# Local attention and a three-weight maxout layer: attention products of two tiles in one insertion, four rotating banks for the unit products, respaced operand steps and a fifth output buffer

## The chip, the cores and the metric

One core of a Trainium2 chip runs the whole program. The metric is the device time of one execution in microseconds; three runs of the kernel before gave 628.42, 628.75 and 629.54 us.

## What is computed

The reference, cut to what matters (8 batches, 8 heads, 576 positions, 64 values a head; 4608 tokens of 512 values):

```python
# attention within chunks of 64 positions
scores = (q_c @ k_c.T) / sqrt(64);  attn = softmax(scores);  x = attn @ v_c
# maxout layer with a hidden width of 768, then the way out
h = max(x @ w1, x @ w2, x @ w3);    out = h @ w_out
```

Everything is float32. Large products are made of three TensorE products of rounded parts (high times low, low times high, high times high).

## The kernel before

**Tiles, groups, units.** The 4608 tokens are 36 tiles of 128. The first eight tiles form two groups of four, whose layer is computed plainly (lines 173 to 175). The other 28 tiles form four *units* of 7, 8, 7 and 6 tiles (numbers 0 to 3; `UNITS`). A unit's layer uses a seven-product scheme for 2 by 2 blocks, so half of a unit's columns (448, 512, 448, 384) is one product's width. All of a unit's products are issued at line 570.

**A unit's hidden layer** (`hidden`, nine steps: three pairs of hidden blocks times w1, w2, w3). A step has seven products of six matmuls, in the order 1, 6, 5, 2, 7, 3, 4. Four of them open a PSUM bank (1, 6, 5, 4); product 2 goes on in the bank of 1, 7 in that of 6, 3 in that of 5, once ScalarE has copied the first content out (line 584, `kept<-pm`). VectorE then reads the finished banks (lines 587 and 581), GpSimd adds copies (594, 590). After the third weight of a pair (steps 3, 6 and 9) the maxima become the operands `Y` of the way out: for each of seven combinations ScalarE writes the rounded part (line 617) and VectorE the rest (line 620).

**A unit's way out** (`project`): 14 products of nine matmuls, in the order 1, 2, 6, 7, 5, 4, 3, each twice (a and b, two halves of the output). Copies of 1 and 6 go through ScalarE (658), product 2's output too (669); the results of 7, 5, 4, 3 through VectorE (661). Outputs are staged in buffers `ao` and stored to `out_t` (653); the buffers rotate over four.

**The next unit's operands** (`operands`, `last_operands`) are made during a way out, with due times counted from 6.5 us after its start: ScalarE rounds (494), VectorE subtracts the rest (498) and makes two differences (489), GpSimd two more (489).

**Attention of a tile** (`plain_steps`): its query and key block is loaded, scores S are 16 products of 64 by 64 blocks (line 223), VectorE takes maxima and subtracts (228, 233), ScalarE the exponential (237), VectorE the sums (181 to 187), GpSimd or VectorE normalises (190), TensorE transposes T in four 128 by 128 pieces (246), ScalarE copies the result (251), and V are 16 products of 64 by 64 blocks with the values (258), which ScalarE copies into the unit's input `stage` (272). Scores and V lie in one pool `ps_s` of two banks, transposes in a bank of their own, `ps_t`.

**What sets the order.** Every step is planned at a due time on a clock `now`, which adds a constant for each three products (`STEP`, `STEP_H`) and for each insertion (`ON_PE`). What is due is issued, so each engine has one fixed order. `tiles(u, time)` inserts unit u's attention work into the products of the unit ahead: at each insertion V of tile n, S of tile n + 2 and T of tile n + 1 stand in a row. Products of the units take their banks from `places`, five in rotation (three of `ps_m`, two of `ps_u`).

Of the kernel before, what the change touches and what calls it, by code (L numbers as in the profile page):

```python
# [9 lines left out]
F32 = mybir.dt.float32  # L10
# [16 lines left out]
UNITS = [7, 8, 7, 6]  # L27
HALF = 512
# [5 lines left out]
ON_PE = {"V": 0.6, "S": 0.6, "T": 0.35}  # L34
# [29 lines left out]
def chunk_attn_maxout_kernel(  # L64
# [138 lines left out]
    def plain_steps(t, x_of, col):  # L203
# [12 lines left out]

        def scores():
            r = st["r"]
            st["s"] = s = bank_of("ps_s")[:, :, t % 2 if t < 4 else 0]
# [23 lines left out]
        def transpose():  # L243
            st["tp"] = tp = ps_t.tile([P, 4, P], F32, name="tp")
            for g in range(4):
                nc.tensor.transpose(out=tp[:, g, :], in_=st["e"][:, g].rearrange("p c k -> p (c k)"),  # L246
                                    identity=ident)

        def transposed():
            st["at"] = xs_p.tile([P, 4, P], F32, name="xs")  # L250
            nc.scalar.copy(out=st["at"], in_=st["tp"])  # L251

        def values():
            st["x"] = x = bank_of("ps_x")[:, :, t % 2] if t < 4 else bank_of("ps_s")[:, :, 1]
# [209 lines left out]
    def unit(t0, count, rooms):  # L464
# [40 lines left out]

        def last_operands():
# [66 lines left out]
        def hidden(n, loads):  # L573
# [31 lines left out]
            if w == 2:  # L605
# [33 lines left out]
        def project(loads):  # L639
# [3 lines left out]
            def store(m, name, make):  # L643
# [40 lines left out]
        return dict(operands=operands, last_operands=last_operands, load=load, load_outer=load_outer, hidden=hidden,  # L684
# [129 lines left out]
    def softmax(n, at, norm):  # L814
# [4 lines left out]
        for name, d in SOFTMAX:  # L819
            plan(at + d, 0.0, lambda name=name: steps(n)[name](*((norm,) if name == "nrm" else ())))  # L820
# [14 lines left out]

    def tiles(u, time):
# [134 lines left out]
```

## Time and profile before

| | |
|---|---|
| median of three runs | 628.75 us |
| the profiled execution | 628.41 us, its span 626.6 us |
| TensorE busy | 613.3 us (98%), weight loads 532.9 us (85%) |
| VectorE, GpSimd, ScalarE busy | 71%, 45%, 44% |
| DMA | 161.26 MB, 73% of the 16 engines' span |
| the chain that ended last | TensorE 82%, VectorE 10%, ScalarE 3% |

The share of TensorE says that it has nearly always a product under way; how long it waited shows only where a product starts later than its spacing to the one ahead. The chain of work gives the places: where it leaves TensorE, another engine held it up.

### The profile page before, as it was taken

Reading aid. Unit: us, or ns where it says so; the run is one execution under the profiler, and the core shown is the slowest. Engines: PE = TensorE matmul, PEld = TensorE weight load, DVE = VectorE, ACT = ScalarE, POOL = GpSimd, SP = SyncE. Lnnn points to the kernel's source line nnn. Section 1 sums busy time; section 2 is a strip of 40 time slices with the busy share of each in tenths; the row PEclk is TensorE's granted clock in tenths of the full one; section 3 lists DMA queues with packets and bytes.
Section 4 is the critical chain, followed back from the end, with each engine's and each line's share of the span. In section 5 each row is a group of like instructions: output and inputs, shape, how many; then the busy total and the mean of one; then the engine's idle time right before and its main releaser. Section 6 shows DMA issues by size and latency. Waiting matters only on the chain.

```text
span 626.6 us, 12688 instructions
## 1 busy us (share of the span) xinstructions
PE 613.3 (98%) x5101; PEld 532.9 (85%) x5102; DVE 446.7 (71%) x684; ACT 272.7 (44%) x483; POOL 281.4 (45%) x235
## 2 busy tenths in 40 slices
PE   7899999999999899999999999999999999999997
PEld 3888888887888789998888888788989999999997
DVE  5898964788756878688659596885488668375752
ACT  4888634345444535353425252533243354232340
POOL 2423577765355765444334443452354334243430
PEclk9999999999999999999999999999999999999999
DMA  8978558685979988575966665759765566977774
GB/s 334 371 291 295 206 186 337 205 282 186 339 230 310 360 308 337 168 259 177 413 244 225 230 203 172 241 190 388 252 223 199 200 200 209 374 263 247 236 233 170
DMA packets 54219, 161.26 MB, mean 257 GB/s; under 512 B 4880, under 2 KB 17168, under 8 KB 49168
## 3 DMA queue, kind: packets, MB, share of 16 engines
q1 hardware_dynamic: 54160, 160.45, 73.0%
q8 instruction: 40, 0.66, 0.4%
q14 instruction: 19, 0.16, 0.1%
HBM read 128.97 MB, written 31.46 MB: 256 GB/s over the span
## 4 chain that ended last, share of the span: by engine, by line
PE 82%; DVE 10%; ACT 3%; issue 3%; DMA 1%; POOL 1%; DVEq 0%; ACTq 0%; POOLq 0%
PE pm L570 57%; PE pm L173 6%; PE pm L174 6%; PE pm L175 6%; PE s L258 3%; PE tp L246 2%; PE s L223 2%; DVE e L233 1%; DVE X L498 1%; DMA out_t<-ao 1%; DVE mx L228 1%; PE pm L736 1%; DVE s L384 1%; DVE sm L181 1%; DVE most L581 1%
## 5 line engine op out<-in xcount | busy, mean ns | idle before, releaser
L570 PE MATMUL pm<-X,ring 128*128 128x448 f32 (+2 forms) x1512 | 311.2, 365 | 2.9 <-ACT kept L584 2.3
L570 PEld LDWEIGHTS pm<-X,ring 128*128 128x128 f32 x1512 | 276.8, 188 | 30.2 <-ACT kept L584 3.6
L584 ACT COPY kept<-pm 128x448 f32<-128x448 f32 (+2 forms) x108 | 57.1, 533 | 135.7 <-PE pm L570 111.8
L570 PE MATMUL pm<-Y,ring 128*128 128x448 f32 (+2 forms) x504 | 103.3, 364 | 1.4 <-ACT kept L658 1.2
L570 PEld LDWEIGHTS pm<-Y,ring 128*128 128x128 f32 x504 | 92.5, 188 | 10.9 <-ACT kept L658 1.9
L581 DVE TENSOR_TENSOR most<-pm,most 128x448 f32<-128x448 f32 (+2 forms) x72 | 44.7, 621 | 44.7 <-PE pm L570 43.5
L594 POOL TENSOR_TENSOR kept<-kept 128x448 f32<-128x448 f32 (+2 forms) x36 | 46.6, 1296 | 61.3 <-ACT kept L584 61.2
L620 DVE TENSOR_TENSOR Y<-most,Y 128x448 fp32r<-128x448 f32 (+2 forms) x72 | 59.1, 840 | 5.4 <-ACT Y L617 5.2
L173 PE MATMUL pm<-xh,wl 128*128 128x512 f32 (+1 forms) x156 | 60.9, 390 | 0.0
L190 POOL TENSOR_TENSOR e<-e,sm 128x512 f32<-128x512 f32 x26 | 27.7, 1066 | 72.8 <-DVE sm L187 53.0
L174 PE MATMUL pm<-xl,wh 128*128 128x512 f32 (+1 forms) x156 | 58.4, 374 | 0.3 <-DVE xl L269 0.3
L175 PE MATMUL pm<-xh,wh 128*128 128x512 f32 (+1 forms) x156 | 58.4, 374 | 0.0
L617 ACT CAST Y<-most 128x448 fp32r<-128x448 f32 (+2 forms) x72 | 40.3, 569 | 37.4 <-DVE most L581 15.5
L590 POOL TENSOR_TENSOR kept<-kept 128x448 f32<-128x448 f32 (+2 forms) x24 | 30.6, 1277 | 48.0 <-DVE kept L587 43.2
L251 ACT COPY xs<-tp 128x512 f32<-128x512 f32 x36 | 21.0, 584 | 48.8 <-PE tp L246 48.7
L228 DVE TENSOR_REDUCE mx<-s 128x8 f32<-128x512 f32 x36 | 24.6, 683 | 20.2 <-PE s L223 20.2
L233 DVE TENSOR_TENSOR e<-s,mx 128x512 f32<-128x512 f32 x36 | 24.8, 690 | 18.1 <-ACT stage L272 17.7
L587 DVE TENSOR_TENSOR kept<-pm,kept 128x448 f32<-128x448 f32 (+2 forms) x36 | 22.3, 619 | 19.8 <-PE pm L570 9.9
L237 ACT ACTIVATE e<-e 128x512 f32<-128x512 f32 x36 | 22.7, 632 | 27.8 <-DVE e L233 27.8
L175 PEld LDWEIGHTS pm<-xh,wh 128*128 128x128 f32 x156 | 29.3, 188 | 5.5
L587 DVE TENSOR_TENSOR pm<-pm,kept 128x448 f32<-128x448 f32 (+2 forms) x48 | 30.1, 627 | 5.5 <-PE pm L570 5.0
L173 PEld LDWEIGHTS pm<-xh,wl 128*128 128x128 f32 x156 | 29.3, 188 | 5.4
(98 smaller groups left out, 853.4 us busy)
## 6 DMA issues: line engine op xcount, KB each, us to landing
ring<-w SPq DMA_DIRECT2D x36, 1024.0 KB, 5.4
ring<-w SPq DMA_DIRECT2D x36, 768.0 KB, 4.7
ring<-wo SPq DMA_DIRECT2D x28, 768.0 KB, 4.6
buf<-in_qk SPq DMA_DIRECT2D x36, 512.0 KB, 6.0
buf<-in_vb SPq DMA_DIRECT2D x36, 256.0 KB, 5.0
w<-s SPq DMA_DIRECT2D x18, 512.0 KB, 4.6
stage<-in_w SPq DMA_DIRECT2D x7, 512.0 KB, 5.7
out_t<-ao SPq DMA_DIRECT2D x16, 224.0 KB, 5.9
```

Source lines behind the costliest of these rows:

```text
L173: nc.tensor.matmul(out=o, lhsT=al, rhs=bh, start=first, stop=False)
L174: nc.tensor.matmul(out=o, lhsT=ah, rhs=bl, start=False, stop=False)
L175: nc.tensor.matmul(out=o, lhsT=ah, rhs=bh, start=False, stop=last)
L228: nc.vector.tensor_reduce(out=st["mx"].rearrange("p (g c) -> p c g", c=2), in_=st["s"], axis=AX.X, op=ALU.max)
L233: nc.vector.tensor_tensor(out=st["e"].rearrange("p g c k -> p c g k"), in0=st["s"], in1=most.unsqueeze(3).broadcast_to([P, 2, 4, 64]), op= ...
L570: nc.tensor.matmul(out=o[i], lhsT=a, rhs=b, start=new and k == 0, stop=last and k == 2, skip_group_check=i in banks_of_product)
L581: return lambda: nc.vector.tensor_tensor(out=M(k, c), in0=of(), in1=M(k, c), op=most)
L584: return lambda: nc.scalar.copy(out=kept(k), in_=o[i])
L587: return lambda: nc.vector.tensor_tensor(out=out(), in0=o[i], in1=kept(k), op=plus)
L594: (0.95, lambda: nc.gpsimd.tensor_tensor(out=kept(2), in0=kept(2), in1=kept(0), op=plus))],
L617: return lambda: nc.scalar.copy(out=y_room(i, jp)[:, 0, :half], in_=t[i]())
L620: return lambda: nc.vector.tensor_tensor(out=y_room(i, jp)[:, 1, :half], in0=t[i](), in1=y_room(i, jp)[:, 0, :half].bitcast(F32), op=minus)
```

## The change

Two tiles of a unit share an insertion from unit 1's tiles on (`pairs`): V of both, then S of the next two. A tile's transposes are planned apart, 9.2 us behind the start of its softmax, and the second tile's softmax begins 0.4 of the distance between insertions later. From tile 17 on (`PAIRED`) a tile's transposes are written over its scores, and tiles of even number use a second pool `ps_y` of two banks. For it `ps_u` is closed at unit 0's start and `ps_t` joins the rotation of the products: four banks in place of five. `ON_PE` is smaller. The operands `Y` of a pair of blocks are due at times that are scaled with the unit's step, numbers 7, 6 and 4 later than before; a unit's operands for the units 1 to 3 have a new order (`operands_behind`). The output buffers rotate over five.

```diff
-ON_PE = {"V": 0.6, "S": 0.6, "T": 0.35}
+PAIRED = sum(GROUPS) + UNITS[0] + 2
+ON_PE = {"V": 0.53, "S": 0.53, "T": 0.36}
...
+        def home(first):
+            return bank_of("ps_y" if t >= first and t % 2 == 0 else "ps_s")
...
-            st["s"] = s = bank_of("ps_s")[:, :, t % 2 if t < 4 else 0]
+            st["s"] = s = home(PAIRED)[:, :, t % 2 if t < 4 else 0]
...
+            if t < PAIRED:
+                st["tp"] = ps_t.tile([P, 512], F32, name="tp", tag="tp").rearrange("p (c x) -> p c x", c=2)
+            else:
+                st["tp"] = st["s"].rearrange("p c g k -> p c (g k)")
...
-            st["x"] = x = bank_of("ps_x")[:, :, t % 2] if t < 4 else bank_of("ps_s")[:, :, 1]
+            st["x"] = x = bank_of("ps_x")[:, :, t % 2] if t < 4 else home(PAIRED - 2)[:, :, 1]
...
+        def operands_behind():
+
+            return [(0.1, high(1)), (1.3, low(1)), (2.5, mix(5, b12, b11, nc.vector)), (2.5, mix(7, b22, b12, nc.gpsimd)),
+                    (3.6, mix(6, b22, source[5], nc.vector)), (4.4, high(5)), (5.5, low(5)), (6.3, high(6)),
+                    (6.7, mix(4, b21, source[6], nc.gpsimd)), (7.2, high(2)), (7.4, low(6)), (8.2, high(7)), (8.5, low(2)),
+                    (9.7, low(7))]
...
+                f, last = STEP_H[count] / STEP_H[7], jp == 2
-                             (2.6, low(5)), (3.1, high(2)), (3.7, low(2)), (3.72, less(nc.gpsimd, t[4], lambda: M(1, 0), t[6])),
-                             (3.75, high(6)), (4.4, low(6)), (4.6, high(7)), (5.2, low(7)), (5.7, high(4)), (6.5, low(4)),
-                             (6.9 if jp == 2 else 5.1, high(3)), (7.5 if jp == 2 else 5.9, low(3))]
+                             (2.6, low(5)), (3.0, high(2)), (3.6, low(2)),
+                             (3.62, less(nc.gpsimd, t[4], lambda: M(1, 0), t[6])),
+                             (6.9 if last else 5.2 * f, high(3)), (7.5 if last else 5.9 * f, low(3)),
+                             (5.8 * f, high(7)), (6.5 * f, low(7)), (6.4 * f, high(6)), (7.1 * f, low(6)),
+                             (7.0 * f, high(4)), (7.7 * f, low(4))]
...
-                    st["o"] = ao_p.tile([P, HALF], F32, name="ao", tag=f"ao{len(outputs) % 4}")[:, :half]
+                    st["o"] = ao_p.tile([P, HALF], F32, name="ao", tag=f"ao{len(outputs) % 5}")[:, :half]
...
-        lead = 14.0 if u == 1 else 20.0
-        gap = (time - 10.0 - lead) / (UNITS[u] - 1)
-        for k in range(UNITS[u]):
-            n, at = sum(UNITS[:u]) + k, now + lead + gap * k
-            insert(at, (("V", n), ("S", n + 2), ("T", n + 1)))
...
+        own = pairs[u - 1]
+        nexts = own[1:] + (pairs[u][:1] if u < len(pairs) else [[]])
+        lead = 20.5 if u == 1 else 20.0
+        gap = (time - 10.0 - lead) / (len(own) - 1)
...
+        for i, (values, scores) in enumerate(zip(own, nexts)):
+            at = now + lead + gap * i
+            insert(at, [("V", n) for n in values] + [("S", n) for n in scores])
...
+            for k, n in enumerate(scores):
+                begin = 0.8 + 0.4 * gap * k
+                softmax(n, at, nc.gpsimd, begin)
+                transposes(n, at + begin + 9.2)
...
+    def banks_for_pairs():
+        places[:] = [(ps_m, "pm")] * 3 + [(ps_t, "tp")]
+
+        def fn():
+            late["ps_u"].__exit__(None, None, None)
+            ps["ps_y"] = ctx.enter_context(tc.tile_pool(name="ps_y", bufs=1, space=PSUM))
+        plan(now + 1.5, 0.0, fn)
```

Lines of the changed kernel have other numbers: 258 is now 265 (V), 223 now 227 (S), 246 now 253 (T), 570 now 584, 584 now 598, 617 now 631, 494 now 501, 658 now 675, 669 now 686.

TensorE, unit 1's hidden layer: one insertion among the products (`L570`, now `L584`). Before, the V, S and T of three tiles:

```order
L570 MATMUL pm<-X_2265,ring 128x512 x3
L258 MATMUL s<-xs,buf 64x64 x16
L223 MATMUL s<-buf 64x64 x16
L246 MATMUL tp<-ident,e 128x128 x4
L570 MATMUL pm<-X_2265,ring 128x512 x3
L570 MATMUL pm<-X_2275,ring 128x512 x6
```

In the change, V and S of two tiles (in the pools named `s` and `y`) and, some products behind, the T of one:

```order
L265 MATMUL s<-xs,buf 64x64 x16
L265 MATMUL y<-xs,buf 64x64 x16
L227 MATMUL s<-buf 64x64 x16
L227 MATMUL y<-buf 64x64 x16
L584 MATMUL pm<-X_2139,ring 128x512 x3
L584 MATMUL pm<-X_2164,ring 128x512 x6
L584 MATMUL pm<-X_2187,ring 128x512 x6
L584 MATMUL pm<-X_2234,ring 128x512 x6
L584 MATMUL pm<-X_2247,ring 128x512 x6
L584 MATMUL pm<-X_2106,ring 128x512 x6
L584 MATMUL pm<-X_2151,ring 128x512 x3
L253 MATMUL s<-ident,e 128x128 x4
```

The insertion has four blocks of 64 by 64 products in a row, and no transpose; the transposes stand alone among products.

ScalarE, unit 0, the fourth step, in which the first `Y` are made (`kept<-pm` are the copies that TensorE waits for, `e<-e` an exponential, `xs<-tp` the copy of transposes, `stage<-s` that of V, `so<-c` a weight for storing). Before:

```order
L584 COPY kept<-pm 128x448
L251 COPY xs<-tp 128x512
L617 CAST Y<-most 128x448
L272 COPY stage<-s 128x2x4x64
L617 CAST Y<-most 128x448
L237 ACTIVATE e<-e 128x512
L617 CAST Y<-m 128x448
L584 COPY kept<-pm 128x448
L617 CAST Y<-most 128x448
L438 CAST so<-c 128x4x256
L617 CAST Y<-most 128x448
L584 COPY kept<-pm 128x448
```

In the change:

```order
L241 ACTIVATE e<-e 128x512
L598 COPY kept<-pm 128x448
L631 CAST Y<-most 128x448
L598 COPY kept<-pm 128x448
L631 CAST Y<-most 128x448
L598 COPY kept<-pm 128x448
L445 CAST so<-c 128x4x256
L613 COPY most<-pm 128x448
```

Between the three copies stood five `Y`, two attention copies, an exponential and `so<-c`; now two `Y` stand there, and the exponential is ahead of them.

ScalarE, the way out of unit 1, where the next unit's operands are made (`X<-stage`, `X<-most`; the copies `kept<-pm` are those of product 6, a and b). Before:

```order
L617 CAST Y<-most 128x512 x2
L669 COPY ao<-pm 128x512
L494 CAST X_2111<-stage 128x2x448
L617 CAST Y<-most 128x512
L669 COPY ao<-pm 128x512
L494 CAST X_2143<-most 128x2x448
L658 COPY kept<-pm 128x512
L494 CAST X_2153<-most 128x2x448
L494 CAST X_2162<-stage 128x2x448
L658 COPY kept<-pm 128x512
L494 CAST X_2183<-stage 128x2x448
```

In the change:

```order
L501 CAST X_2106<-stage 128x2x448
L686 COPY ao<-pm 128x512
L631 CAST Y<-most 128x512
L241 ACTIVATE e<-e 128x512
L631 CAST Y<-m 128x512
L631 CAST Y<-most 128x512
L686 COPY ao<-pm 128x512
L675 COPY kept<-pm 128x512
L501 CAST X_2139<-most 128x2x448
L501 CAST X_2151<-most 128x2x448
L675 COPY kept<-pm 128x512
L501 CAST X_2164<-stage 128x2x448
```

The first copy has moved ahead of the rounding of operand 5 (X_2143, now X_2139); the second stands behind the rounding of operands 5 and 6 as before (X_2153, now X_2151), and no longer behind operand 2's (X_2162, now X_2164). An exponential and three `Y` stand between X_2106 and the first copy, where one `Y` stood between X_2111 and X_2143.

## Rows read from the trace of the kernel before

**Rows 1.** The first line of the page.

```profile
span 626.6 us, 12688 instructions
```

**Rows 2.** Of the chain of work that ended last (start us, us, what), two unbroken runs of products, of 448 and of 384 columns.

```profile
258.39 26.15 PE pm L570 x129
537.74 85.57 PE pm L570 x492
```

**Rows 3.** TensorE alone in order of time, in five windows in the units: start us, us, engine, line, operation, names, shapes and count; in brackets the idle time before a row and what ended it.

```profile
198.65 3.90 PE L570 MATMUL pm<-X,ring 128*128 128x448 f32 x18
203.14 6.34 PE L570 MATMUL pm<-X,ring 128*128 128x448 f32 x30 [0.60 <-ACT kept L584]
...
209.42 0.69 PE L258 MATMUL s<-xs,buf 64*64 64x64 f32 x32
...
210.92 3.89 PE L570 MATMUL pm<-X,ring 128*128 128x448 f32 x18
215.65 1.49 PE L570 MATMUL pm<-X,ring 128*128 128x448 f32 x6 [0.84 <-ACT kept L584]
217.96 1.28 PE L570 MATMUL pm<-X,ring 128*128 128x448 f32 x5 [0.82 <-ACT kept L584]
...
292.04 1.47 PE L570 MATMUL pm<-Y,ring 128*128 128x448 f32 x6
293.69 2.50 PE L570 MATMUL pm<-Y,ring 128*128 128x448 f32 x11 [0.18 <-DVE ao L661]
...
393.43 12.40 PE L570 MATMUL pm<-Y,ring 128*128 128x512 f32 x54
407.03 3.13 PE L570 MATMUL pm<-Y,ring 128*128 128x512 f32 x12 [1.19 <-ACT kept L658]
...
534.85 2.27 PE L570 MATMUL pm<-X,ring 128*128 128x384 f32 x12
537.74 2.53 PE L570 MATMUL pm<-X,ring 128*128 128x384 f32 x13 [0.62 <-DVE ao L661]
```

**Rows 4.** All engines in order of time in unit 0 (window 196 to 219), ScalarE's rows.

```profile
202.04 0.63 ACT L237 ACTIVATE e<-e 128x512 f32<-128x512 f32 x1 [0.76 <-DVE e L233]
202.58 1.38 ACT L584 COPY kept<-pm 128x448 f32<-128x448 f32 x3
...
215.08 0.52 ACT L584 COPY kept<-pm 128x448 f32<-128x448 f32 x1
```

**Rows 5.** The same view at the passage from unit 1 to unit 2.

```profile
405.55 0.94 ACT L494 CAST X<-most 128x896 fp32r<-128x896 f32 x1 [2.27 <-DVE most L489]
...
406.40 0.58 ACT L658 COPY kept<-pm 128x512 f32<-128x512 f32 x1
```

**Rows 6.** The same view at the passage from unit 2 to unit 3 (SPq issues the DMAs).

```profile
530.02 0.34 SPq L653 DMA_DIRECT2D out_t<-ao  x1
...
537.06 0.63 DVE L661 TENSOR_TENSOR ao<-pm,kept 128x448 f32<-128x448 f32 x1 [3.21 <-DMA out_t<-ao]
```

**Rows 7.** TensorE alone in order of time (window 305 to 325): two insertions in unit 1's hidden layer.

```profile
306.40 0.69 PE L258 MATMUL s<-xs,buf 64*64 64x64 f32 x32
...
307.91 13.88 PE L570 MATMUL pm<-X,ring 128*128 128x512 f32 x60
321.72 0.69 PE L258 MATMUL s<-xs,buf 64*64 64x64 f32 x32
```

**Rows 8.** The same view (window 122 to 127) in the second group of plain tokens, with 512-column products.

```profile
122.89 0.39 PE L175 MATMUL pm<-xh,wh 128*128 128x512 f32 x1
...
124.30 0.50 PE L173 MATMUL pm<-xh,wl 128*128 128x512 f32 x1
124.64 0.39 PE L174 MATMUL pm<-xl,wh 128*128 128x512 f32 x1
...
125.57 0.39 PE L175 MATMUL pm<-xh,wh 128*128 128x512 f32 x1
125.80 0.60 PE L246 MATMUL tp<-ident,e 128*128 128x128 f32 x4
...
126.47 0.40 PE L174 MATMUL pm<-xl,wh 128*128 128x512 f32 x1
```

**Rows 9.** GpSimd (window 217 to 221): the latest normalisation of a tile in the units; its scores belong to the insertion at 209.42 in group 3.

```profile
218.23 1.25 POOL L190 TENSOR_TENSOR e<-e,sm 128x512 f32<-128x512 f32 x1 [0.94 <-DVE sm L187]
```

**Rows 10.** The passage from unit 0 to unit 1: TensorE's first product of unit 1 (window 296 to 302) and VectorE's last outputs (window 294 to 303).

```profile
297.45 4.72 PE L570 MATMUL pm<-X,ring 128*128 128x512 f32 x20
...
298.47 0.58 DVE L661 TENSOR_TENSOR ao<-pm,kept 128x448 f32<-128x448 f32 x1
300.12 0.62 DVE L661 TENSOR_TENSOR ao<-pm,kept 128x448 f32<-128x448 f32 x1 [1.07 <-DMA out_t<-ao]
```

**Rows 11.** VectorE and GpSimd at the subtractions of unit 1's input, all engines in order of time.

```profile
279.71 2.10 POOL L664 TENSOR_TENSOR kept<-kept 128x448 f32<-128x448 f32 x1 [4.16 <-ACT kept L658]
280.83 2.07 DVE L489 TENSOR_TENSOR most<-stage,most 128x1024 f32<-128x1024 f32 x1
281.77 3.40 POOL L489 TENSOR_TENSOR stage<-stage 128x1024 f32<-128x1024 f32 x1
```

**Rows 12.** Unit 2, the fourth step of its hidden layer and the start of the fifth (window 454 to 468): TensorE, and the VectorE sum that frees the bank of product 7.

```profile
453.81 13.64 PE L570 MATMUL pm<-X,ring 128*128 128x448 f32 x65
...
464.66 0.61 DVE L587 TENSOR_TENSOR kept<-pm,kept 128x448 f32<-128x448 f32 x1
```

More of the change, by code (lines that the diff above doesn't have):

```diff
@@ L250, in transposed @@
             st["at"] = xs_p.tile([P, 4, P], F32, name="xs")
-            nc.scalar.copy(out=st["at"], in_=st["tp"])
+            nc.scalar.copy(out=st["at"].rearrange("p (c g) x -> p c (g x)", c=2), in_=st["tp"])
         def values():
-            st["x"] = x = bank_of("ps_x")[:, :, t % 2] if t < 4 else bank_of("ps_s")[:, :, 1]
+            st["x"] = x = bank_of("ps_x")[:, :, t % 2] if t < 4 else home(PAIRED - 2)[:, :, 1]
             for g in range(4):
@@ L812, in insert, with softmax @@
                 plan(at, ON_PE[name], lambda name=name, n=n: steps(n)[name]())
-    def softmax(n, at, norm):
+    def softmax(n, at, norm, begin=0.0):
         if n >= tiles_in_units:
@@ L819, in softmax @@
         for name, d in SOFTMAX:
-            plan(at + d, 0.0, lambda name=name: steps(n)[name](*((norm,) if name == "nrm" else ())))
+            plan(at + begin + d, 0.0, lambda name=name: steps(n)[name](*((norm,) if name == "nrm" else ())))
     def first_tiles(time):
@@ L834, in first_tiles, with transposes @@
                 plan(at + 1.0, 0.0, lambda n=n: steps(n - 2)["x"]())
+    pairs = []
+    for u, count in enumerate(UNITS[1:]):
+        ns = range(sum(UNITS[:u + 1]), sum(UNITS[:u + 2]))
+        pairs.append([list(ns[k:k + 2]) for k in range(0, count, 2)])
+    def transposes(n, at):
+        insert(at, (("T", n),))
+        if n < tiles_in_units:
+            plan(at + 0.5, 0.0, lambda: steps(n)["at"]())
     def tiles(u, time):
@@ L838, in tiles @@
             return
-        lead = 14.0 if u == 1 else 20.0
-        gap = (time - 10.0 - lead) / (UNITS[u] - 1)
-        for k in range(UNITS[u]):
-            n, at = sum(UNITS[:u]) + k, now + lead + gap * k
-            insert(at, (("V", n), ("S", n + 2), ("T", n + 1)))
-            softmax(n + 2, at, nc.gpsimd)
-            plan(at - 16.0, 0.0, lambda n=n: steps(n)["v"]())
-            plan(at + 1.0, 0.0, lambda n=n: steps(n)["x"]())
-            if n + 1 < tiles_in_units:
-                plan(at + 0.9, 0.0, lambda n=n: steps(n + 1)["at"]())
+        own = pairs[u - 1]
+        nexts = own[1:] + (pairs[u][:1] if u < len(pairs) else [[]])
+        lead = 20.5 if u == 1 else 20.0
+        gap = (time - 10.0 - lead) / (len(own) - 1)
+        if u == 1:
+            transposes(own[0][1], now + 9.0)
+        for i, (values, scores) in enumerate(zip(own, nexts)):
+            at = now + lead + gap * i
+            insert(at, [("V", n) for n in values] + [("S", n) for n in scores])
+            for k, n in enumerate(values):
+                plan(at - 16.0 + 2.0 * k, 0.0, lambda n=n: steps(n)["v"]())
+                plan(at + 1.0 + 0.7 * k, 0.0, lambda n=n: steps(n)["x"]())
+            for k, n in enumerate(scores):
+                begin = 0.8 + 0.4 * gap * k
+                softmax(n, at, nc.gpsimd, begin)
+                transposes(n, at + begin + 9.2)
     def stores():
@@ L861, in operands @@
         if u < len(units):
-            for at, fn in units[u][0]["operands"]():
+            for at, fn in units[u][0]["operands_behind" if u else "operands"]():
                 plan(now + begin + at, 0.0, fn)
@@ L908, in chunk_attn_maxout_kernel @@
     parts += [("steps", lambda: g["project"](0, 1)), ("steps", lambda: g["project"](2)), ("steps", lambda: g["project"](3))]
+    parts.append(("do", lambda: banks_for_pairs()))
     for u, (it, t0, count) in enumerate(units):
@@ L919, in more_banks @@
         first_x.__exit__(None, None, None)
-        ps_u = ctx.enter_context(tc.tile_pool(name="ps_u", bufs=2, space=PSUM))
+        late["ps_u"] = tc.tile_pool(name="ps_u", bufs=2, space=PSUM)
+        ps_u = late["ps_u"].__enter__()
         places.extend([(ps_m, "pm")] * 3 + [(ps_u, "pu")] * 2)
```

5 lines of the change are left out of this document (2 added, 3 removed).

## The prediction, on record before the result

> **What bounds the kernel now.** I read the page first, then the waits of TensorE, then TensorE in order of time, and the other engines around each place where it starts late. The span is 626.6 us [rows 1], and the profiled execution took 628.41 us, 1.8 us more; the median of the runs, 628.75 us, is 0.34 us above it. I sum against 628.41 and add 0.34 at the end. About 0.2% (1.3 us) is what a measurement of this kernel can tell from no change.
>
> TensorE is the bound: the reader is to see in the chain that its products follow each other for long stretches at one spacing: 26.15 us for 129 products of 448 columns is 0.203 us each, 85.57 us for 492 of 384 columns is 0.174 us [rows 2], and 54 of 512 columns take 12.40 us with the tail of the last [rows 3]; for these I use the planner's own step, 0.6815 us for three, 0.227 us each. So only two things can shorten the units: cheaper insertions of attention work, and fewer late starts. A late start is a row that begins after the start of the row ahead plus its count times the spacing. There are six in the units [rows 3]: 203.14 (0.84 us late, since 198.65 + 18 x 0.203 = 202.30), 215.65 (1.08), 217.96 (1.09), 293.69 (0.43), 407.03 (1.34) and 537.74 (0.80), together 5.6 us. What held each of them up:
>
> - The three in unit 0 wait for ScalarE's copies (`kept`). At 202.04 an exponential stood ahead of them on ScalarE, itself waiting for VectorE, and the copies came out in one block from 202.58; at 215.08 the copy came behind the conversions of `Y`, whose rounding at 214.62 was just ahead of it [rows 4].
> - 407.03, in the way out of unit 1, waits for the copy of product 6 at 406.40. Ahead of it on ScalarE stood the rounding of operand 5, which waited 2.27 us for VectorE's difference [rows 5].
> - 537.74, at the start of unit 3, waits for unit 2's last output, and that had waited 3.21 us for a store to free its buffer [rows 6]. 293.69 waits for an output that VectorE made late.
>
> **The change part by part.**
>
> *Insertions.* Now V, S and T of one tile in a row cost 321.72 - 306.40 = 15.32 us less 60 products, 13.62 us: 1.70 us [rows 7]. V and S alone cost 124.64 - 122.89 = 1.75 us less two products, 1.30 us, and T alone between products 126.47 - 125.57 = 0.90 us less two, 0.45 us [rows 8]. So T behind S cost 0.40 us, and taking it out costs 0.05 us for each of 20 tiles, +1.0 us. In return the passage from the 128 by 128 products to the 64 by 64 ones and back is made 11 times and not 21. Its price is the part of the 1.30 us that the two blocks do not need. The trace has no pair of insertions in one, so I bound it by the parts: from 64 by 64 blocks to the next product and on to the one behind takes 124.64 - 124.30 = 0.34 us in place of 0.227, 0.11 us; entry and the step out of the last block I put at 0.08 to 0.1 us each, an estimate from what is left of the 1.30 us beside two blocks of about 0.5 us. That is 0.25 to 0.32 us, times 10: 2.5 to 3.2 us. Less 1.0: **1.5 to 2.2 us gained; I take 1.9**, near the upper end, since both edges are seen to cost at a full passage.
>
> *T moved.* T is now due 10.0 us behind an insertion's start for the first tile, 9.2 us behind the softmax's for the second. The latest normalisation in the units ended at 219.48, 10.06 us behind its insertion at 209.42 [rows 3, 9]. So one T of about 20 would have waited, by some 0.1 us: between 0 and 1 us, I take 0.1. A T that waits holds all products behind it.
>
> *`Y` spread.* In unit 0's fourth step the copies leave the crowd: the order shows two `Y` between the three copies, where five, an exponential and a weight cast stood. The three late starts there (3.0 us) can all go, or stay because the same VectorE work is only elsewhere: 0 to 3.0 us. I take 2.6, nearer to all, because the exponential that blocked at 202.04 and the `Y` that blocked at 215.08 are both off those places. Where a stall goes, the next thing late is VectorE's sums, which have three products (3.6 us) of slack with four banks.
>
> The other side of the spread is the way out. There, the rest of `Y` for product 6 is due 7.1 us (times the step's ratio) behind its start, where it was due at 4.4, and its first use is in the last third of the fifth product, 4 x 9 + 6 = 42 products on: 8.5 us at 0.203. The work itself is off the path with about 0.7 us to spare, and in unit 1, where a softmax now stands among it on both engines, I reckon it 0.0 to 0.6 us late: +0.1 in the sum.
>
> *New operand order.* Operand 5 is rounded 1.0 us later on the clock, so the copy of product 6 a goes ahead of it: the 1.34 us of 407.03 fall away. But everything on ScalarE there is later by the `Y` put in front, and the copy of 6 b still stands behind operand 5, in unit 1 behind operand 6 as well, and those wait for VectorE's differences. In unit 1 I put that wait between 0 and 3.0 us (operand 6's difference behind GpSimd, below) and take 1.5 for the passage, +0.2 on before. At 0 to 1 the copy of 6 b is needed 7 x 9 products after the start, 12.8 us; VectorE's difference now comes behind `Y` that are due up to 2.7 us later than they were (4.4 to 7.1), of which I count 1.5 us: 0.43 before becomes 1.0, +0.6, with bounds of -0.4 and +1.9 (below).
>
> *Fifth output buffer and four banks.* The last output of unit 2 waited for the store of the output four ahead; it now waits for the one five ahead, issued at 530.02 [rows 6]. If that also takes until about 536, some 1 us goes. But with four banks in rotation the second product of the next unit needs that output's bank, not the third: one product (6 x 0.174 = 1.04 us) earlier. The two cancel: -0.1, between -0.8 and +1.0. Within the steps four banks are enough: four are opened a step, and each comes round a whole step later.
>
> Sum: -1.9 + 0.1 - 2.6 + 0.1 + 0.2 + 0.6 - 0.1 = -3.6. 628.41 - 3.6 = 624.8, and with 0.34 **625.1 us**.
>
> **The rivals.**
>
> *R1, the late starts all go.* For it: each has a named cause that the change touches. Against: three causes are only moved by a place or two. 628.41 - 1.9 - 5.6 + 0.34 = 621.3 us.
>
> *R2, only the insertions pay.* VectorE's amount of work is unchanged, and what waits for it waits elsewhere. 628.41 - 1.9 + 0.34 = 626.9 us.
>
> *R3, GpSimd gets in first.* On VectorE, operand 6's difference no longer stands right behind operand 5's in unit 1: two small softmax steps come between. GpSimd's difference needs only the first. The rows show what follows when GpSimd is first: a difference took 2.07 us from 280.83, until 1.09 us after GpSimd's operation from 279.71 ended at 281.81; and GpSimd's next, from 281.77, took 3.40 us, as VectorE was first there [rows 11]. So operand 6's difference would come about 2 us late, and with it the copy of 6 b: the passage 1 to 2 costs 3.0 us, and with late `Y` 0.6 more. 624.8 + 1.5 + 0.5 + 0.34 = 627.1 us. The Trainium skill, page "SBUF — State Buffer", section "Who interferes with whom", states it as a rule: VectorE and GpSimd share a pair of ports that one of them holds for its whole instruction, and a VectorE operation with two SBUF inputs contends with GpSimd's reads. By that rule, the trace agrees, moving GpSimd's differences ahead buys VectorE nothing.
>
> *R4, slower: four banks.* The mechanism is VectorE's lateness at a unit's end. The last two outputs of unit 0 ended at 299.05 and 300.74, and unit 1's first product began at 297.45 [rows 10]. With four banks that product waits for the first of them (1.6 us), and the second, due 1.36 us on at 300.41, waits for the other (0.3): 1.9. At unit 3's start, +1.0 as above. And in unit 2's fourth step the sum of product 7 ended at 465.27, while the second product of the next step began about 44 + 6 products behind 453.81, at 463.96 [rows 12]: 1.3 us. If VectorE stays as late as that and unit 0's stalls only change place, 628.41 - 1.9 + 1.9 + 1.0 + 1.3 = 630.7, with 0.34 631.1 us. The point from which it decides: a unit's last output later than about one product (1.2 us) behind TensorE. Against it: `Y` is spread, and the operand chain starts GpSimd's differences earlier.
>
> **How the numbers follow.** Forecast 0.50, by its terms 623.5 to 626.6; R1 0.18; R2 0.14; R3 0.11; R4 0.07. The time is the forecast's, 625.1 us. The range is to leave out at most 2 in 10: half of R1 below and R4 with some of R3 above. 621.8 to 627.6 us. Faster by over 0.2% (under 627.5): forecast 0.49, R1 0.18, R2 0.11, R3 0.05: 0.83. Within 0.2%: 0.11. Slower: R4's 0.06.
>
> **What would show it.** Right: 11 blocks of V and S in the units, about 2.3 us each with two tiles, and T alone at 0.45 us; no late start in unit 0's third to fifth step; late starts of 1 to 2 us in the ways out, named after ScalarE's copy of product 6 or after VectorE's outputs. Wrong: a block of two tiles at 2.6 us or more (nothing gained by sharing); transposes that wait for GpSimd's normalisation; TensorE waiting for VectorE at the second or third product of a unit or of the steps behind `Y` (R4); a late start over 2 us in unit 1's way out (R3); no late start left over 0.3 us (R1).

## The result, and the profile after

The changed kernel takes **632.55 us** (median of six runs, 630.77 to 633.23), the kernel before 628.87 us (628.42 to 630.46): ratio 1.0051, 95% interval 1.0035 to 1.0068. It is slower, outside the range of 621.8 to 627.6 us. The profiled execution took 632.87 us, 4.46 us more than that of before.

The page of the changed kernel shows its span, to be set against [rows 1], and the shares of the chain that ended last (before: TensorE 82%, VectorE 10%).

```profile
span 631.1 us, 12694 instructions
...
PE 73%; DVE 18%; ACT 3%; issue 3%; POOL 2%; DVEq 0%; POOLq 0%; ACTq 0%
```

VectorE's share of the chain has nearly doubled. TensorE in order of time (start us, us, engine, line, operation, shapes, count; in brackets the idle time before a row and what ended it), the lines that answer to [rows 3] and [rows 7]:

```profile
217.49 6.20 PE L584 MATMUL pm<-X,ring 128*128 128x448 f32 x27
224.85 3.91 PE L584 MATMUL pm<-X,ring 128*128 128x448 f32 x18 [1.16 <-ACT kept L598]
...
243.16 8.27 PE L584 MATMUL pm<-X,ring 128*128 128x448 f32 x39
252.90 1.48 PE L584 MATMUL pm<-X,ring 128*128 128x448 f32 x6 [1.46 <-DVE most L601]
...
319.75 4.70 PE L584 MATMUL pm<-X,ring 128*128 128x512 f32 x20
324.38 0.69 PE L265 MATMUL s<-xs,buf 64*64 64x64 f32 x32
...
326.40 8.46 PE L584 MATMUL pm<-X,ring 128*128 128x512 f32 x36
...
404.65 5.34 PE L584 MATMUL pm<-Y,ring 128*128 128x512 f32 x22
412.21 0.69 PE L253 MATMUL s<-ident,e 128*128 128x128 f32 x4 [2.23 <-POOL e L191]
412.63 7.99 PE L584 MATMUL pm<-Y,ring 128*128 128x512 f32 x27
...
491.71 6.33 PE L584 MATMUL pm<-X,ring 128*128 128x448 f32 x30
498.58 1.70 PE L584 MATMUL pm<-X,ring 128*128 128x448 f32 x7 [0.53 <-DVE most L601]
...
533.83 6.52 PE L584 MATMUL pm<-Y,ring 128*128 128x448 f32 x31
540.19 5.02 PE L584 MATMUL pm<-X,ring 128*128 128x384 f32 x28
```

The reader is to see three things. The block of two tiles is cheap: 326.40 - 319.75 less 20 x 0.227 is 2.11 us, with 0.11 more until the second product 2.22 us, where two insertions of before, which held two T as well, cost 3.4. Unit 3 starts without a wait (540.19, before 0.80 us late). And new late starts stand behind VectorE, ScalarE and GpSimd: 224.85, 252.90, 498.58 and, before a transpose, 412.21. Unit 1's way out is the worst place. All engines there:

```profile
407.01 1.09 DVE L496 TENSOR_TENSOR most<-stage 128x896 f32<-128x896 f32 x1
...
408.19 2.12 POOL L496 TENSOR_TENSOR stage<-stage 128x896 f32<-128x896 f32 x1 [5.66 <-DVE sm L185]
408.22 0.20 DVE L188 RECIPROCAL sm<-sm 128x8 f32<-128x8 f32 x1
408.34 2.92 DVE L496 TENSOR_TENSOR most<-stage,most 128x896 f32<-128x896 f32 x1
...
410.27 1.89 POOL L191 TENSOR_TENSOR e<-e,sm 128x512 f32<-128x512 f32 x1
...
411.29 0.94 ACT L501 CAST X<-most 128x896 fp32r<-128x896 f32 x1 [2.20 <-DVE most L496]
...
412.14 0.58 ACT L675 COPY kept<-pm 128x512 f32<-128x512 f32 x1
```

GpSimd's difference for operand 7 starts while VectorE does two small softmax steps; VectorE's difference for operand 6 then takes 2.92 us in place of 1.09, and two things are late behind these two: the normalisation at 410.27, for which the transposes wait, and ScalarE's rounding at 411.29, behind which the copy of product 6 b stands. Three windows there, with their length, the busy time of TensorE, of its weight loads, of VectorE, ScalarE and GpSimd (instructions in brackets), then the granted TensorE clock, the DMA share and GB/s:

```profile
410.00:412.20 2.20, 0.00 (x0) 0.00 (x0) 2.20 (x2) 0.91 (x2) 2.20 (x3) 1.00 1.05 407
412.60:416.20 3.60, 3.60 (x12) 2.83 (x11) 3.60 (x3) 2.28 (x4) 3.60 (x2) 0.53 0.14 53
416.50:419.00 2.50, 2.50 (x13) 2.05 (x12) 2.50 (x3) 0.00 (x0) 2.50 (x2) 1.00 0.26 44
```

Behind the wait the granted clock is at its lower level, 1.2 GHz: products at 0.427 us in place of 0.227, by these spacings some 1.7 us lost over the next nine products. Five of the six runs have a mean clock of 0.997 and spans of 630.4 to 631.5 us; the sixth has 1.000 and 629.0. By that one run (630.77 us) about half of the 3.7 us lost goes with the clock.

**The account.** Lateness of a part is its time less its products at the spacings of [rows 2, 3] and less its insertions at their undisturbed costs (1.68 us V, S and T, 2.22 two tiles, 1.76 three of the four blocks, 0.44 T alone, 1.22 V and T, 1.28 two V, 0.82 V; the trace shows each). All in us, of the profiled executions:

| | before | after | difference | forecast |
|---|---|---|---|---|
| insertions | 33.98 | 31.43 | -2.55 | -1.9 |
| unit 0, steps | 2.91 | 4.24 | +1.33 | -2.6 |
| unit 0, way out | 0.39 | 1.84 | +1.45 | +0.6 |
| unit 1, steps | 0.02 | 0.85 | +0.83 | 0 |
| unit 1, way out | 1.57 | 4.31 | +2.74 | +0.4 |
| unit 2, steps | 0.15 | 0.94 | +0.79 | 0 |
| unit 2, way out, and unit 3 | 0.63 | -0.20 | -0.83 | -0.1 |
| the two groups | | | +0.66 | 0 |

Sum +4.42, forecast -3.6. (The last row's part differs as much between profiled executions in which the groups' code is the same: unit 0 starts at 177.65 us in kernel 7 below and at 179.21 in kernel 14.)

One part of unit 0's 4.24 waits for no engine: inside the second block of two tiles there is a pause, which the view puts to `issue`. It makes that block 0.62 us longer than the others, and in the other kernels with pairs 0.11 to 0.82 us. What it is stays open.

```profile
208.32 0.27 PE L227 MATMUL y<-buf 64*64 64x64 f32 x1 [0.35 <-issue]
```

### The profile page after: what moved, and what is told of

Its sections match the earlier page's. It is cut to its first block, busy times and chain, and to the rows that moved or that the text cites. A ratio compares the mean times of both kernels' runs of the same rounds, so it can differ in the third digit from the quotient of the medians.

```text
span 631.1 us, 12694 instructions
## 1 busy us (share of the span) xinstructions
PE 615.1 (97%) x5102; PEld 533.7 (85%) x5102; DVE 445.7 (71%) x684; ACT 272.0 (43%) x483; POOL 278.6 (44%) x235
## 4 chain that ended last, share of the span: by engine, by line
PE 73%; DVE 18%; ACT 3%; issue 3%; POOL 2%; DVEq 0%; POOLq 0%; ACTq 0%
PE pm L584 52%; PE pm L174 5%; PE pm L175 5%; PE pm L176 5%; DVE Y L634 4%; DVE e L237 2%; DVE mx L232 1%; DVE sm L182 1%; PE s L265 1%; PE s L227 1%; DVE most L595 1%; DVE sm L185 1%; DVE s L391 1%; DVE X L505 1%; ACT e L241 1%
## 5 line engine op out<-in xcount | busy, mean ns | idle before, releaser
L584 PE MATMUL pm<-X,ring 128*128 128x448 f32 (+2 forms) x1512 | 313.6, 366 | 3.4 <-DVE most L601 2.0
L584 PEld LDWEIGHTS pm<-X,ring 128*128 128x128 f32 x1512 | 276.2, 188 | 31.9 <-DVE most L601 4.2
L584 PE MATMUL pm<-Y,ring 128*128 128x448 f32 (+2 forms) x504 | 106.5, 370 | 1.0 <-DVE kept L678 0.4
L584 PEld LDWEIGHTS pm<-Y,ring 128*128 128x128 f32 x504 | 93.2, 190 | 11.4 <-DVE Y L634 1.1
L175 PEld LDWEIGHTS pm<-xl,wh 128*128 128x128 f32 x156 | 29.4, 189 | 5.2 <-DVE xl L276 0.5
L232 DVE TENSOR_REDUCE mx<-s 128x8 f32<-128x512 f32 x27 | 18.4, 683 | 20.8 <-ACT stage L279 12.1
L182 DVE TENSOR_REDUCE sm<-e 128x8 f32<-128x512 f32 x36 | 24.5, 681 | 7.1 <-ACT e L241 6.6
```

What stands on the lines that cost most here:

```text
L175: nc.tensor.matmul(out=o, lhsT=ah, rhs=bl, start=False, stop=False)
L182: nc.vector.tensor_reduce(out=sm, in_=e, axis=AX.X, op=ALU.add)
L584: nc.tensor.matmul(out=o[i], lhsT=a, rhs=b, start=new and k == 0, stop=last and k == 2, skip_group_check=i in banks_of_product)
```

## The experiments

The theory from this trace: the loss is VectorE's and GpSimd's lateness in two places, unit 1's way out (N) and the steps behind `Y` (Y). Rivals: the four banks (B), and a lateness that is only handed on (P). Lateness by part is worked out in the same way. The ratios, with 95% intervals, are to runs of the kernel before beside each kernel, whose medians were 628.31 us (kernels 1 to 4), 628.45 (5 to 8), 628.76 (9, 10, 13, 14) and 628.59 (11, 12):

| kernel | median us | ratio | u0 steps | out 0 | u1 steps | out 1 | u2 steps | out 2, u3 |
|---|---|---|---|---|---|---|---|---|
| before | 628.87 | 1 | 2.91 | 0.39 | 0.02 | 1.57 | 0.15 | 0.63 |
| after | 632.55 | 1.0051 (1.0035 to 1.0068) | 4.24 | 1.84 | 0.85 | 4.31 | 0.94 | -0.20 |
| 1 t_later | 631.70 | 1.0047 (1.0031 to 1.0063) | 4.23 | 1.84 | 0.86 | 2.69 | 0.93 | -0.21 |
| 2 diff7_later | 630.16 | 1.0025 (1.0016 to 1.0034) | 4.22 | 2.17 | 0.88 | 0.85 | 0.92 | 0.87 |
| 3 a_old_operands | 632.54 | 1.0063 (1.0046 to 1.0080) | 4.40 | 3.42 | 0.88 | 1.58 | 0.91 | 0.88 |
| 4 a_old_y | 630.95 | 1.0036 (1.0024 to 1.0049) | 2.93 | 2.06 | 0.76 | 3.32 | 0.43 | -0.26 |
| 5 combo1 | 627.96 | 0.9983 (0.9970 to 0.9996) | 3.00 | 2.07 | 0.74 | 1.46 | 0.43 | -0.27 |
| 6 y_only | 630.84 | 1.0033 (1.0019 to 1.0047) | 2.01 | 1.80 | 0.02 | 2.41 | -0.16 | 1.75 |
| 7 operands_only | 626.67 | 0.9970 (0.9951 to 0.9990) | 2.93 | 0.44 | 0.04 | -0.03 | 0.15 | 0.94 |
| 8 four_banks | 632.29 | 1.0050 (1.0031 to 1.0069) | 3.46 | 0.39 | 1.04 | 1.57 | 1.37 | 0.72 |
| 9 pairs_only | 633.07 | 1.0064 (1.0045 to 1.0083) | 3.03 | 5.05 | 0.72 | 2.14 | 0.43 | 0.53 |
| 10 combo2 | 627.74 | 0.9979 (0.9968 to 0.9989) | 2.99 | 2.16 | 0.82 | 1.42 | 0.64 | -0.27 |
| 11 early_softmax | 627.66 | 0.9985 (0.9975 to 0.9995) | 2.92 | 1.00 | 0.79 | 2.18 | 0.45 | -0.26 |
| 12 no_softmax | 626.39 | 0.9961 (0.9947 to 0.9975) | 2.92 | 0.17 | 0.77 | 0.21 | 0.45 | 1.35 |
| 13 before_order_buffer | 626.02 | 0.9960 (0.9947 to 0.9974) | 3.00 | 0.44 | 0.04 | -0.03 | 0.12 | -0.26 |
| 14 before_order_buffer_y | 625.10 | 0.9937 (0.9920 to 0.9954) | 1.98 | 0.37 | 0.02 | -0.03 | -0.16 | -0.27 |

Kernels 1 to 5 and 9 to 12 have the insertions of the change (31.4 us), the others those of before (34.0).

**1. The late transposes, due later.**

```diff
-                transposes(n, at + begin + 9.2)
+                late_t = 3.0 if u == 2 and i == len(own) - 1 and k else 0.0
+                transposes(n, at + begin + 9.2 + late_t)
```

> In the changed kernel, the transposes of the last tile in unit 1's way out start 2.4 us late (412.21), behind GpSimd's normalisation, and the products behind them run for some 4 us at a spacing of 0.427 us in place of 0.227, with a granted clock of 0.50. Here these transposes and their copy alone are due 3.0 us later. Theory N (that wait, and the clock that falls behind it, are the largest single loss): the wait goes, the clock stays at 1.00, the time falls by 2.4 + 1.9 = 4.3 us to about 628.3. Rival P (VectorE and GpSimd are late there, and the next thing that needs them waits in place of the transposes): the late start moves to the copy or the product behind, the time stays within 1 us of 632.5.

The rival held. The transposes wait no more, but the product behind the copy of 6 b does. TensorE in order of time:

```profile
405.82 4.25 PE L584 MATMUL pm<-Y,ring 128*128 128x512 f32 x18
412.17 2.34 PE L584 MATMUL pm<-Y,ring 128*128 128x512 f32 x9 [2.10 <-ACT kept L675]
```

Two waits lay over each other; taking one away shows the other, 2.26 us against 2.39. What fell away in the profile is the stretch at the lower clock; three of the six runs still have a mean clock of 0.997, and where it fell in them is not on record.

**2. GpSimd's difference for operand 7, due later**, nothing else.

```diff
-            return [(0.1, high(1)), (1.3, low(1)), (2.5, mix(5, b12, b11, nc.vector)), (2.5, mix(7, b22, b12, nc.gpsimd)),
-                    (3.6, mix(6, b22, source[5], nc.vector)), (4.4, high(5)), (5.5, low(5)), (6.3, high(6)),
+            return [(0.1, high(1)), (1.3, low(1)), (2.5, mix(5, b12, b11, nc.vector)),
+                    (3.6, mix(6, b22, source[5], nc.vector)), (4.4, high(5)), (4.6, mix(7, b22, b12, nc.gpsimd)), (5.5, low(5)), (6.3, high(6)),
```

> The changed kernel with one entry moved: GpSimd's difference for operand 7 is due at 4.6 in place of 2.5. Order of TensorE, VectorE and ScalarE is the same; on GpSimd the normalisation in unit 1's way out now stands ahead of that difference, and in the other two ways out the difference stands one sum later. Theory N, with the operand order as its cause: the normalisation starts at VectorE's reciprocal (408.4) and not 1.9 us later, the transposes wait 0 to 1 us, the clock holds: 628.3 to 629.5 us. Rival P (it is VectorE's own difference, 2.9 us long, that slows the normalisation): the wait stays over 1.5 us and the time above 631.

Theory N held for unit 1's way out: 4.31 to 0.85. All engines there:

```profile
408.06 1.04 DVE L496 TENSOR_TENSOR most<-stage,most 128x896 f32<-128x896 f32 x1
408.31 1.69 POOL L191 TENSOR_TENSOR e<-e,sm 128x512 f32<-128x512 f32 x1 [6.07 <-DVE sm L188]
...
410.05 0.66 PE L253 MATMUL s<-ident,e 128*128 128x128 f32 x4 [0.35 <-POOL e L191]
```

VectorE's difference takes 1.04 us again, since it starts ahead of GpSimd, and both waits are gone but for 0.5. The time is 0.7 above the expectation, because the same edit made unit 2's way out 1.1 us worse, where no softmax stands.

**3. The old operand order in the changed kernel** (`"operands"` for all units in place of `"operands_behind" if u else "operands"`).

> The changed kernel with the operand order of the kernel before. If the new order is to blame for the late transposes (theory N): they wait under 1 us, as the normalisation is ahead of GpSimd's differences; but the wait for the copy of product 6 in the way out, 1.3 us before, comes back: 628.5 to 630. If the order is not to blame (rival P): 631.5 to 634.

The time is the rival's, the reason is not. Unit 1's way out improves from 4.31 to 1.58, so the order was to blame there; but the other two get worse by 1.6 and 1.1 us. On the whole the new order is no loss even here.

**4. The old times of `Y` in the changed kernel** (the lines with `-` in the change's diff of `after[4]`, back).

> The changed kernel with the times of Y of the kernel before. Theory Y (Y spread behind VectorE's sums makes the steps behind it late: 224.85, 252.90 and 498.58, 3.6 us together): these three get shorter by 2 us or more in sum, and others come back at the fourth step; 630 to 632. Rival B (four rotating banks with any crowded step; the place of Y does not matter): as late as before or later, at the same or the neighbouring products, 632 to 635.

Theory Y held: unit 0's steps fall from 4.24 to 2.93, which is the value of before, unit 2's from 0.94 to 0.43. TensorE, the place of 252.90:

```profile
249.63 1.49 PE L584 MATMUL pm<-X,ring 128*128 128x448 f32 x6 [0.65 <-DVE kept L601]
251.51 1.49 PE L584 MATMUL pm<-X,ring 128*128 128x448 f32 x6 [0.39 <-DVE most L601]
```

Two things speak for rival B beside it. The late starts that are left wait for VectorE's sums, at second and third products of the fifth and eighth step, where the kernel before has none. And the three late starts of unit 0 that the prediction gave to `Y` (203.14, 215.65 and 217.96 before) are not here either, though `Y` has its old times; nor are they in kernel 9. TensorE in the same stretch, with the first late start at its end:

```profile
208.52 8.78 PE L584 MATMUL pm<-X,ring 128*128 128x448 f32 x42
...
217.49 2.07 PE L584 MATMUL pm<-X,ring 128*128 128x448 f32 x9
219.83 6.37 PE L584 MATMUL pm<-X,ring 128*128 128x448 f32 x29 [0.27 <-DVE kept L601]
```

**5. Both**: old times of `Y`, and GpSimd's difference at 4.6 in unit 2's operands alone (`4.6 if count == 7 else 2.5`).

> The changed kernel with the times of Y of the kernel before and, for the passage from unit 1 to unit 2 alone, GpSimd's difference for operand 7 due at 4.6 in place of 2.5. Each alone gave 1.6 and 2.4 us, by medians against 632.55. If they are two separate causes, both come off: 628.5 us, with unit 1's way out within 1.5 us of the kernel before (changed kernel: +4.6) and unit 0's steps within 0.5 us (+1.6). If both were one lateness of VectorE, handed on: 630 to 631.

Two separate causes: 627.96, a little below the expectation and 0.2% under the kernel before.

**6 to 8. Each part alone, on the kernel before**: the new times of `Y`; the new operand order; four rotating banks:

```diff
-        ps_u = ctx.enter_context(tc.tile_pool(name="ps_u", bufs=2, space=PSUM))
-        places.extend([(ps_m, "pm")] * 3 + [(ps_u, "pu")] * 2)
+        ps_u, ps_v = (ctx.enter_context(tc.tile_pool(name=n, bufs=1, space=PSUM)) for n in ("ps_u", "ps_v"))
+        places.extend([(ps_m, "pm")] * 3 + [(ps_u, "pu"), (ps_v, "pv")])
...
+        places.pop()
```

> The kernel before with the new times of Y alone (no pairs, five banks in the steps, old operand order). The prediction's term: the three late starts of unit 0's fourth step go, 2.6 us gained, less 0.5 for late outputs in the ways out: 626.2 against 628.3. Theory Y (the spread moves VectorE's lateness into the step behind, and the ways out wait): 628 to 630, with new late starts in the steps behind Y. Rival B (only with four banks does it cost): 626 to 628.

> The kernel before with the new operand order alone. The prediction's terms: 0 to 1 +0.6, 1 to 2 +0.2: 629.1 against 628.3. Theory N (the order costs much only with a softmax of a pair between the two differences of VectorE): unit 1's way out within 1 us of the kernel before, 627.5 to 629. Rival O (GpSimd's difference gets in first with or without that softmax): unit 1's way out 2 us longer or more, 630 or more.

> The kernel before with four rotating banks in the units in place of five, and nothing else. Rival B (R4 of the prediction, the four banks): new late starts of 1 us and more at the second products of the steps behind Y and at the unit's starts, 630 to 632.5. Theory Y (the four banks are enough for VectorE's lateness as it was before; only the way the pairs crowd it matters): up to 1 us at unit 3's start, up to 0.5 elsewhere, 628.3 to 629.8.

`Y` alone: 0.9 gained in unit 0's steps, and 1.4, 0.8 and 1.1 lost in the ways out and at unit 3. That is theory Y's loss, somewhat above its figure, but only in the ways out: the new late starts that it expected in the steps do not come with five banks. The three late starts of unit 0 stay, two of them shorter:

```profile
203.81 6.36 PE L570 MATMUL pm<-X,ring 128*128 128x448 f32 x30 [0.61 <-ACT kept L584]
...
215.86 1.49 PE L570 MATMUL pm<-X,ring 128*128 128x448 f32 x6 [0.37 <-ACT kept L584]
217.71 2.50 PE L570 MATMUL pm<-X,ring 128*128 128x448 f32 x11 [0.35 <-ACT kept L584]
```

The order alone: 1.6 us gained in unit 1's way out, better than the prediction and than theory N. With no softmax step between its differences VectorE's second one starts 0.04 us ahead of GpSimd's and takes 1.09 us:

```profile
404.95 1.09 DVE L489 TENSOR_TENSOR most<-stage,most 128x896 f32<-128x896 f32 x1
404.99 3.04 POOL L489 TENSOR_TENSOR stage<-stage 128x896 f32<-128x896 f32 x1 [5.30 <-DVE most L489]
```

The four banks alone: **3.8 us by the medians, rival B**. TensorE, at unit 1's start and from the fourth to the fifth step of unit 2:

```profile
298.46 1.54 PE L570 MATMUL pm<-X,ring 128*128 128x512 f32 x6
300.21 5.15 PE L570 MATMUL pm<-X,ring 128*128 128x512 f32 x20 [0.21 <-DVE ao L661]
...
454.82 11.37 PE L570 MATMUL pm<-X,ring 128*128 128x448 f32 x55
467.34 2.94 PE L570 MATMUL pm<-X,ring 128*128 128x448 f32 x13 [1.15 <-DVE kept L587]
```

467.34 starts 1.30 us later than its spacing behind the product ahead, the figure that R4 worked out from [rows 12]. At unit 1's start R4 was too high: the first product does not wait and the second is 0.4 us late, where R4 had 1.9 for the two. By the profile the parts sum to 2.9 us (8.54 against 5.68 in all). Three of the six runs have a mean clock of 0.997, as six of the 24 of the kernel before beside them; the others alone give 3.4 us (631.52 against 628.17).

**9. Pairs without the other parts** (the edits of 3 and 4, and four output buffers).

> The changed kernel without three of its parts: old times of Y, old operand order, four output buffers; what is left is the products of two tiles in one insertion, the softmax and transposes of the second tile, and the four banks. If the parts add up (insertions -2.55, four banks +3.8 by the medians): 629.7 us. If the crowded second softmax costs besides, in the ways out (theory N: with the old order, 2.6 us late in unit 0's way out and 1.2 in unit 1's): 631 to 632.5.

Not additive: 633.07, 0.6 us above theory N's range. In unit 0's way out a product is 2.77 us late: the copy it waits for stands behind two roundings on ScalarE, and these behind VectorE's differences. The clock falls behind that wait. TensorE, and a window behind it:

```profile
279.65 4.42 PE L584 MATMUL pm<-Y,ring 128*128 128x448 f32 x21
286.67 8.55 PE L584 MATMUL pm<-Y,ring 128*128 128x448 f32 x34 [2.61 <-ACT kept L672]
```

```profile
286.60:290.00 3.40, 3.33 (x10) 3.00 (x11) 3.40 (x3) 1.92 (x3) 2.81 (x2) 0.57 0.06 21
```

**10. Kernel 5 with the transposes later too** (edit 1 with 1.6 us).

> The changed kernel with old times of Y, GpSimd's difference for operand 7 later in the passage 1 to 2, and there the transposes and copy of the last tile 1.6 us later too. In the kernel without that last edit they waited 1.32 us. If nothing else is late there: 1.2 us less than its 627.96, 626.8 us. Rival P: the copy of product 6 is late as well and takes its place: within 0.6 us of 627.96.

Rival P again, with the copy 1.20 us late: 627.74.

**11 and 12. The softmax among the operands.** In kernel 5, the second tile of each unit's last pair: its softmax ahead of the way out (`begin = 5.0 * k` for the last pair), and left out but for the exponential, for units 0 and 1.

> The changed kernel with old times of Y and GpSimd's difference for operand 7 later (627.96), and the second tile's softmax and transposes of each unit's last pair 5.0 us behind the block, right behind the first tile's, and so ahead of the way out in place of inside it. Theory N (it is that softmax among the operands that makes the ways out long): no transposes wait in unit 1's way out, unit 0's is 1 us and unit 1's 1.5 to 2 us shorter; the step ahead may lose some 0.5; 625.5 to 626.5. Rival P (VectorE has no room ahead of the way out either): Y comes late in place of it, 627.5 to 629.

> The same kernel (627.96), but for the second tile of the last pair of units 0 and 1 the softmax is left out but for its exponential: no maximum, difference, sum, guard, reciprocal or normalisation on VectorE and GpSimd, which is some 3.5 us of VectorE's and 1.2 to 1.9 us of GpSimd's work each. Theory N: this work is all that lengthens the ways out: unit 0's falls from +2.7 to +1.0 or so, unit 1's from +1.8 to -1.5 (as the new order alone has it); 623 to 625. If something else of the pairs does it (rival): the ways out stay over +2 and +1, 627 to 628.

Without that work both ways out are on time (0.17 and 0.21 us late): theory N. TensorE in unit 1's way out, no wait in brackets:

```profile
394.62 10.60 PE L588 MATMUL pm<-Y,ring 128*128 128x512 f32 x46
405.06 0.60 PE L257 MATMUL s<-ident,e 128*128 128x128 f32 x4
405.42 6.53 PE L588 MATMUL pm<-Y,ring 128*128 128x512 f32 x27
```

The time, 626.39, is above the expectation; 1.5 us came back at unit 3's start, behind a load of weights. Moved ahead, the softmax frees unit 0's way out by half and makes unit 1's worse (2.18): VectorE has no room there either, as it works without a pause from 389.81 to 402.80 us, and 627.66 is the rival's figure.

**13 and 14. What is left of the change without pairs.** The kernel before with the new order and five output buffers, and with the new times of `Y` for the first two thirds besides (operand 2's, 0.1 us earlier, in all three):

```diff
+                after[4] += [(3.75, high(6)), (4.4, low(6)), (4.6, high(7)), (5.2, low(7)), (5.7, high(4)), (6.5, low(4)),
+                             (6.9, high(3)), (7.5, low(3))] if last else [
+                             (5.2 * f, high(3)), (5.9 * f, low(3)), (5.8 * f, high(7)), (6.5 * f, low(7)),
+                             (6.4 * f, high(6)), (7.1 * f, low(6)), (7.0 * f, high(4)), (7.7 * f, low(4))]
```

> The kernel before with the new operand order and the fifth output buffer, nothing else. The order alone gave 626.67. The late start at unit 3's first products (1.07 us there) waits for an output that waits for a store's buffer: with a fifth buffer it goes to 0.1 or so, 625.7 us, if the store is the cause; if VectorE is, 626.7.

> As the kernel before with the new operand order and the fifth buffer, and the new times of Y for the first two thirds of a unit alone; the last third, which runs into the way out, keeps the old times. Y alone took 0.9 us off unit 0's steps and 0.3 off unit 2's and gave 3.1 us back in the ways out. If the loss in the ways out comes from the last third's Y alone: 1.2 us less than the kernel without Y, 624.5 us. If the first two thirds hand their lateness on as well: as much as without or more, 625.7 to 627.

The first: unit 3's start, 1.07 us late with four buffers, is on time; the store was the cause. TensorE there:

```profile
529.65 3.81 PE L577 MATMUL pm<-Y,ring 128*128 128x448 f32 x18
533.29 11.97 PE L577 MATMUL pm<-X,ring 128*128 128x384 f32 x68
```

The second, **625.10 us**, beats both kernels: the ways out keep their times and the steps their gain. Its chain that ended last:

```profile
PE 89%; DVE 7%; ACT 2%; issue 1%; DVEq 0%; ACTq 0%
```

## Why the prediction was wrong, step by step

- **Insertions**: right, and more than said: -2.55 for -1.9. The block of two tiles costs 2.22 us, where 2.3 was forecast.
- **`Y` spread** is the step that failed most: -2.6 became +1.33. "Nearer to all" was the wrong choice between 0 and 3.0, and the cause was wrong too. The three late starts did go, but the pairs took them away: kernels 4 and 9 lack them with the old times of `Y`, kernel 8 keeps them with four banks and no pairs, and kernel 6 keeps all three with the new `Y`, for a gain of 0.9. In the changed kernel the spread costs 1.3 us there (4.24 against 2.93 in kernel 4), since the second tile's softmax and VectorE's sums stand in the steps behind, where VectorE now also has `Y` to do. The slack of three products that was given to the sums was not there: 252.90 and 498.58 wait for them. At 224.85 an exponential that waits for VectorE stands ahead of ScalarE's copies, the very pattern of [rows 4] in another place:

```profile
223.75 0.63 ACT L241 ACTIVATE e<-e 128x512 f32<-128x512 f32 x1 [3.59 <-DVE e L237]
224.28 0.95 ACT L598 COPY kept<-pm 128x448 f32<-128x448 f32 x2
```

- **Four banks** (R4, given 0.07): "within the steps four banks are enough" failed. Kernel 8 has 1.04 and 1.37 us of lateness in unit 1's and 2's steps with the banks as its only edit. I had worked the 1.3 us out and then let a gain in `Y` excuse it. The changed kernel's 0.83 and 0.79 there are of like size, but not at the same products: units 1 and 3 start without a wait, and 498.58 is a third product of the eighth step, which is on time again with the old `Y` (kernel 4: 0.43 in all). Kernel 6, with the new `Y` and five banks, has no such late start. No kernel has the pairs with five banks, so how the lateness in the steps is shared between the banks and the pairs is not shown.
- **The passage 1 to 2** (R3, given 0.11): its mechanism is what happened, GpSimd first at 408.19 and VectorE's difference 2.92 us long, as in [rows 11]; R3's price of 3.0 us for the passage stands beside 2.4 us of waiting and 1.7 more by the clock, which no term had. The Trainium skill, page "SBUF — State Buffer", section "Who interferes with whom", says that a VectorE operation with two SBUF inputs contends with GpSimd's reads, and that the order of issue decides who blocks; the trace agrees: 2.92 us behind GpSimd, 1.04 ahead of it (kernel 2).
- **T waits on its norm**, +0.1: the wait is 2.4 us, but kernel 1 shows that the product behind would have waited as long. I took the latest normalisation from a trace in which no difference of GpSimd's stood ahead of one.
- **0 to 1**: +1.45 for +0.6, inside the bounds I gave. Kernel 12 shows the pair's softmax in it; kernels 6 and 14 together show that the last third of `Y` has such an effect too (1.80 with it, 0.37 without).
- **Operand order**: forecast a loss of 0.8, alone it gains (kernel 7).
- **Fifth buffer**: the cancelling -0.1 was -0.83. The store was all of that wait (kernel 13), and four banks do not bring it forward by a product: in kernel 8 it is still the third product of unit 3 that starts late (541.04, behind 12 matmuls from 538.10).

The forecast treated R3 and R4 as alternatives to it and to each other. They are separate places on one VectorE that was busy 71% before and after, and lateness came at both.

On the whole the insertions gave 2.55 us and lateness in the units took 6.31. (By parts the insertions fell in unit 1's and 2's steps and rose in the ways out of units 0 and 1, where some of the blocks and transposes now stand.) Kernel 10, by its ratio the best with pairs that does all the work, is still 1.7 us above kernel 13 without them, on the same chip. What stays open, besides the share of the banks, is what decides whether the clock falls.

## What to carry to other kernels

Merging TensorE work saves what the insertion costs and bunches the work of the engines behind it; price the bunch where those engines are busiest, and add up the rivals that sit in different places. Before two late things are mended, look what else is late at the same moment: an edit that takes away one wait of two shows the other (kernel 1). Slack in PSUM banks is worth its measured time: one bank of five was worth more here (2.9 us by parts) than all insertions saved (2.55).

## What the runs showed of the hardware that was not expected

After a wait of 2.23 us (changed kernel) and of 2.61 us (kernel 9) TensorE's granted clock stood at 0.53 and 0.57 over the next 3.6 and 3.4 us. By the spacing of the products that cost about 1.7 us (0.427 us in place of 0.227) and 1.4 us (0.373 in place of 0.203). After 2.10 us (kernel 1) and 3.01 us (kernel 4), in the profiled executions, it stayed at 1.00:

```profile
411.56 0.66 PE L253 MATMUL s<-ident,e 128*128 128x128 f32 x4 [3.01 <-POOL e L191]
411.97 3.25 PE L584 MATMUL pm<-Y,ring 128*128 128x512 f32 x13
```

Thirteen products in 3.25 us there are at full clock. Kernels 1 and 4 have other runs with a mean clock of 0.997. So has the kernel before: nine of its 83 runs beside these kernels, at 630.0 to 630.7 us, though in its profile TensorE waits for another engine nowhere longer than 1.5 us. The length of the wait alone does not tell, and where the clock fell in those runs is not on record.
